# Attention and two expert layers in emulated fp32: another gate function in the first layer, four operand rooms in its second product, later weight sets

## The chip, the cores and the metric

The kernel runs on one core of a Trainium2 chip. A core has TensorE (PE, matmuls into PSUM, the accumulator memory of eight banks), VectorE (DVE), ScalarE (ACT), GpSimd (POOL) and SyncE (SP), which here issues all DMAs, in one queue. The metric is the time of one execution on the device, in microseconds; lower is better.

## The reference

An attention over a compressed memory, then two expert layers, on 8 batches x 576 positions = 4608 tokens of width 512.

```python
# q, k, v: (8, 8, 576, 64); phi: (8, 8, 576, 32); all float32
a = exp(phi - max(phi, axis=2)); a /= sum(a, axis=2) + 1e-9
k_m = einsum('bhsm,bhsd->bhmd', a, k);  v_m = einsum('bhsm,bhsd->bhmd', a, v)
scores = q @ k_m.T / sqrt(64)
attn = softmax(scores, axis=-1);        x = attn @ v_m      # -> (4608, 512)
# layer 1: w_in (512, 2048), w_out (2048, 512), float64
h = x @ w_in;  g = h * sigmoid(1.702 * h);  x = g @ w_out
# layer 2: the same shapes, its own weights
h = x @ w_in;  g = h * sigmoid(h);          out = g @ w_out
```

## The kernel before, in words

Every product is done as three matmuls of a high and a low part (`PASSES`: high x high, high x low, low x high); a tile's high part is a rounded copy made by ACT, its low part the difference, made by DVE or POOL. The weights come as float64 and are converted on the chip: ACT scales both halves (`wconv0`), DVE shifts and sets the sign, POOL adds (`wconv1`). There are four large products, one behind the other.

**First product** (`first1`, 256 steps, 32 a batch). Not attn·v_m and then w_in, but w' = v_m·w_in is made per batch (`wp_mm`, four sets of 512 columns, tiles `slab`) and multiplied with the softmax (`attnT`). A step is six matmuls of 288 columns into one of four PSUM banks, then the gate: ACT takes Tanh of 0.851 h (L326), DVE forms (tanh + 1)·h (L327), which is twice h·sigmoid(1.702 h). Each pair of steps fills one of five `g` buffers, which `g_store` sends to `gs` in DRAM. Between the steps stands the attention of the next batch (`plan_attention`): max over phi, exp of phi (L186), the k/v product (`kv_mm`, 144 matmuls in the trace), transposes of q, the scores, and their softmax with its exp (L270); and the w' sets (`plan_wprime`: matmuls, then `wp_hi` on ACT and `wp_lo` on DVE). Each piece is put in a list under a step number and a place in the step: "e" ahead of the step's matmuls, "p" and "l" behind them, "d" for DMAs. The loop over the steps emits these lists, and the order of each engine's queue is the order of emission. Nothing else decides it.

**Second product** (`first2`, 168 units of 12 matmuls of 384 columns). It is a Strassen-Winograd form: seven products for each of six blocks of 768 tokens, four units (quarters of the inner dimension) a product. A unit's left operand is made from fetched `g` tiles (`r`, `rr`, four quadrants of a block) by `a_prep`: an ACT cast (high part) and a DVE difference (low part, L64) into one of `ROOMS`. Two of the first product's three rooms lie where the attention's buffers were, the third (`op3`) over the first product's `slab` and `g` buffers. `make(0, ROOMS[0], t + 2)` stands ahead of unit t. Results leave through `evac2` (ACT copy times 0.25, DVE sum) to `xs` in DRAM.

**Third product** (`step1`, 48 steps of seven products, L604), gated by one ACT instruction, Silu (L614). **Fourth product** (`prod2`, L666), which is the second's form with other operands, made three units ahead; its fourth quadrant's `r` tiles are fetched ahead of its loop, behind the third product.

The second layer's weights are converted during the second and third product, sent to DRAM (`w2s`), fetched again as sums of blocks (`w_fetch`) and made into seven tiles a set (`w_sums`, `w_high`, `w_low`). Sets (0,0) and (0,1) of the third product are made in the second's last 28 units (`LAST`), (0,2) and (0,3) in the third product. The first layer's `w_out` is loaded and converted in the first product (`w_convert`); its last set goes through `wos` tiles and `wo_move`.

On SP each DMA waits for the DMA eight before it, so the order of issue matters there as it does on the engines.

## Time and profile before

| | |
|---|---|
| time, median of 3 runs | 1513.67 us (1511.62 to 1515.62) |
| profiled execution, its own time | 1512.86 us |
| its span | 1511.1 us |
| PE busy | 1415.0 us, 94% |
| PE weight loads busy | 1334.0 us, 88% |
| DVE busy | 1046.9 us, 69% |
| ACT busy | 788.8 us, 52% |
| POOL busy | 216.1 us, 14% |

The span is the time from the first to the last instruction of the profiled execution; the rest of its own time lies around it. "Busy" is the sum over an engine's instructions. A TensorE that waits inside a stream for its operands, or runs at a lower granted clock, counts as busy in long entries, so 94% isn't 94% of its peak: a stretch has to be compared with the same matmuls in a stretch that waits for nothing. The first product takes the span's first 393.7 us, the second the next 393.8, the third 356, the fourth the rest.

### The profile page before, as it was taken

How to read it: one execution, taken by the hardware profiler on the slowest of the kernel's cores; microseconds unless marked ns; L12 is line 12 of the kernel's file. 1: busy time of each engine (PE TensorE's matmuls, PEld its weight loads, DVE VectorE, ACT ScalarE, POOL GpSimd, SP SyncE). 2: the span in 40 equal slices, each digit the busy share in tenths (PEclk: the TensorE clock that was granted, in tenths of full speed). 3: DMA queues.
4: the chain of work that ended last, by engine and by line, in shares of the span. 5: the costliest groups of instructions: out<-in, count | busy, mean ns of one | idle time of the engine just before them, and what ended most of it. 6: DMA issues, size and time to landing. Idle time of an engine off the chain costs nothing.

```text
span 1511.1 us, 27760 instructions
## 1 busy us (share of the span) xinstructions
PE 1415.0 (94%) x10776; PEld 1334.0 (88%) x10776; DVE 1046.9 (69%) x1513; ACT 788.8 (52%) x1408; POOL 216.1 (14%) x209
## 2 busy tenths in 40 slices
...
GB/s 307 183 189 210 270 246 231 263 174 174 281 35 224 166 158 261 101 223 202 80 99 165 191 194 215 152 212 200 136 210 183 198 43 178 172 50 199 114 107 33
DMA packets 195300, 265.54 MB, mean 176 GB/s; under 512 B 50528, under 2 KB 158048, under 8 KB 195168
## 3 DMA queue, kind: packets, MB, share of 16 engines
...
q8 instruction: 84, 1.38, 0.4%
q14 instruction: 48, 0.39, 0.1%
...
## 4 chain that ended last, share of the span: by engine, by line
PE 69%; DVE 12%; DMA 5%; ACT 5%; issue 4%; POOL 1%; SPq 1%; ACTq 0%; DVEq 0%; POOLq 0%
PE p L666 23%; PE xb L604 13%; PE p L516 12%; PE y L604 10%; PE h L321 8%; DVE op L64 4%; DMA gs<-g 2%; PE aa L240 2%; DVE rr L64 2%; ACT op L499 1%; PE a L196 1%; DMA rr<-gs 1%; DVE o L531 1%; ACT g L326 1%; DVE r L64 1%
## 5 line engine op out<-in xcount | busy, mean ns | idle before, releaser
L516 PE MATMUL p<-op,wq 128*128 128x384 f32 x2016 | 366.1, 341 | 28.0 <-ACT op L499 16.7
L516 PEld LDWEIGHTS p<-op,wq 128*128 128x128 f32 x2016 | 353.6, 190 | 40.2 <-DVE op L64 20.9
L666 PE MATMUL p<-wq,op 128*128 128x256 f32 x3024 | 360.1, 282 | 5.4 <-ACT o L680 3.0
L666 PEld LDWEIGHTS p<-wq,op 128*128 128x128 f32 x3024 | 359.7, 191 | 6.0 <-ACT o L680 3.2
L499 ACT CAST op<-rr 128x768 fp32r<-128x768 f32 x216 | 178.2, 834 | 199.3 <-PE p L666 80.5
L64 DVE TENSOR_TENSOR op<-rr,op 128x768 fp32r<-128x768 f32 x216 | 210.0, 976 | 93.8 <-ACT op L499 92.8
L321 PEld LDWEIGHTS h<-attnT,slab 128*128 128x128 f32 x1536 | 217.0, 195 | 50.5 <-issue 21.9
L321 PE MATMUL h<-attnT,slab 128*128 128x288 f32 x1536 | 248.3, 312 | 14.0 <-DVE g L327 5.2
L604 PE MATMUL xb<-xq,wq 128*128 128x384 f32 x1152 | 216.5, 336 | 0.9 <-DVE e L61 0.5
L604 PEld LDWEIGHTS xb<-xq,wq 128*128 128x128 f32 x1152 | 201.4, 188 | 1.6 <-DVE e L61 0.8
L327 DVE SCALAR_TENSOR_TENSOR g<-g,h 128x288 f32<-128x288 f32 x256 | 110.7, 445 | 98.5 <-ACT g L326 97.9
L604 PE MATMUL y<-xq,wq 128*128 128x384 f32 x864 | 166.6, 337 | 0.7 <-DVE xq L64 0.6
L64 DVE TENSOR_TENSOR op<-r,op 128x768 fp32r<-128x768 f32 x120 | 116.8, 976 | 59.8 <-ACT op L499 59.7
L499 ACT CAST op<-r 128x768 fp32r<-128x768 f32 x120 | 99.7, 834 | 108.9 <-PE p L666 43.9
L604 PEld LDWEIGHTS y<-xq,wq 128*128 128x128 f32 x864 | 151.7, 188 | 1.5 <-DVE xq L64 0.8
L326 ACT ACTIVATE g<-h 128x288 f32<-128x288 f32 x256 | 102.8, 419 | 90.8 <-PE h L321 70.6
L104 POOL TENSOR_TENSOR wst<-wst 128x512 int32<-128x512 int32 x24 | 34.6, 1443 | 496.5 <-DVE wst L102 422.3
L61 DVE TENSOR_TENSOR e<-e,y 128x384 f32<-128x384 f32 x96 | 52.9, 552 | 60.2 <-PE y L604 56.1
L614 ACT ACTIVATE gq<-e 128x384 f32<-128x384 f32 x144 | 75.8, 527 | 15.0 <-DVE e L61 14.8
L61 DVE TENSOR_TENSOR e<-e,xb 128x384 f32<-128x384 f32 x48 | 26.6, 554 | 76.7 <-PE xb L604 70.9
L427 ACT CAST wq<-wst 128x512 fp32r<-128x512 f32 x83 | 51.1, 617 | 35.3 <-DVE wst L64 20.4
L629 ACT COPY e<-xb 128x384 f32<-128x384 f32 x48 | 23.0, 480 | 57.9 <-PE xb L604 57.9
(117 smaller groups left out, 1290.5 us busy)
## 6 DMA issues: line engine op xcount, KB each, us to landing
rr<-gs SPq DMA_DIRECT2D x120, 384.0 KB, 6.5
gs<-g SPq DMA_DIRECT2D x128, 288.0 KB, 4.1
...
```

Source lines behind the costliest of these rows:

```text
L61: eng.tensor_tensor(out=out, in0=a, in1=b, op=ALU.add)
L64: eng.tensor_tensor(out=out, in0=a, in1=b, op=ALU.subtract)
L104: nc.gpsimd.tensor_tensor(out=z, in0=z, in1=low, op=ALU.add)
L321: nc.tensor.matmul(out=h, lhsT=slab[b, f // 4, g][:, wi, f0:f0 + 128], rhs=x[:, g, xi], start=(g == 0 and n == 0), stop=(g == 1 and n == 2))
L326: nc.scalar.activation(out=t, in_=h, func=ACTF.Tanh, scale=0.851)
L327: nc.vector.scalar_tensor_tensor(out=t, in0=t, scalar=1.0, in1=h, op0=ALU.add, op1=ALU.mult)
L427: nc.scalar.copy(out=t[:, :, 0], in_=wst[m, c, k])
L499: nc.scalar.copy(out=t[:, :, 0], in_=s)
L516: nc.tensor.matmul(out=out[:, d, :HB], lhsT=w[:, s, wi, d * 128:(d + 1) * 128], rhs=t[:, s, gi], start=(start and p == 0 and s == 0 and n ...
L604: nc.tensor.matmul(out=out, lhsT=w[:, s, wi, f0:f0 + 128], rhs=x[:, s, xi], start=(start and s == 0 and n == 0), stop=(s == 1 and n == 2), ...
L614: nc.scalar.activation(out=t, in_=h, func=ACTF.Silu, scale=2.0)
L666: nc.tensor.matmul(out=out[:, d], lhsT=t[:, u, gi, d * 128:(d + 1) * 128], rhs=w[:, u, wi], start=(start and d != 1 and p == 0 and u == 0 ...
```

## The change

- The first layer's gate becomes one ACT instruction, Silu(2x), which gives the twofold gate directly. For that the factor 0.851 (`GATE`) is put into `kv_norm`, and taken out again in the softmax's scale and in the second product's evacuation. Silu and exp (with Tanh) lie in different tables of ACT, so each exp is between two table loads. The two exp of the scores of one batch and the two halves of the next batch's phi exp are put at neighbouring steps; a gate between exps that are at most `gap` = 8 steps apart stays Tanh and product (9 of 256). There are 18 table loads for 2 before.
- All step numbers of the first product stand in one table, `PLAN`, with other values; phi's max, difference and exp go in halves, and the start is one list.
- Fetches for the second product: five in the last steps, six and `wo_move` behind them.
- The second product has four operand rooms for three, makes operands three units ahead for two, and has three output tiles for four.
- Weight set (0,1) is made in the third product's first steps, with it (0,2) and (0,3) and what follows are later; the x blocks are fetched 14 products later.
- Ahead of the fourth product, the fourth quadrant is fetched in the third product's last full step, and the third operand made four products later.

```diff
+    GATE = 1.702 / 2
...
-        nc.scalar.activation(out=t, in_=h, func=ACTF.Tanh, scale=0.851)
-        nc.vector.scalar_tensor_tensor(out=t, in0=t, scalar=1.0, in1=h, op0=ALU.add, op1=ALU.mult)
+        if any(lo <= u < hi for lo, hi in exps):
+            nc.scalar.activation(out=t, in_=h, func=ACTF.Tanh)
+            nc.vector.scalar_tensor_tensor(out=t, in0=t, scalar=1.0, in1=h, op0=ALU.add, op1=ALU.mult)
+        else:
+            nc.scalar.activation(out=t, in_=h, func=ACTF.Silu, scale=2.0)
...
-        return pools["mb"].tile([128, 2, HB], F32, tag="o", name="o2", bufs=4)
+        return pools["mb"].tile([128, 2, HB], F32, tag="o", name="o2", bufs=3)
...
-        nc.scalar.activation(out=out, in_=a[:, :, :HB], func=ACTF.Copy, scale=0.25)
+        nc.scalar.activation(out=out, in_=a[:, :, :HB], func=ACTF.Copy, scale=0.25 / GATE)
...
+             3: {'phi': [-29, -28],
+                 'kv': [-35, -32, -29, -26, -23, -21, -14, -14],
+                 'pm': [-25, -25],
+                 'mt': -22,
+                 'mr': -21,
+                 'mb': -21,
+                 'sb': [-19, -18],
+                 'ex': [-17, -16],
+                 'es': -14,
+                 'mm': -4,
...
+                    [[151, 150, 157, 160], [156, 159, 165, 167], 173], [[216, 218, 222, 225], [222, 224, 227, 230], -3]],
+             'w3': [6, 6, 7, 7],
...
+             'rf': [19, 20, 21, 22, 23, 2],
...
+             'w0': [3, 4, 5, 6, 7, 8, 9, 1, 3, 5, 7, 9, 11, 13, 16, 18, 20, 22, 24, 26, 28, 30, 32, 34, 36, 38, 40, 42],
+             'wf': [0, 11, 1, 15],
...
+        if fn in (phi_exp, soft_exp, OPS["ex"], OPS["exp"]):
+            near = [x for x in exps if x[0] - PLAN["gap"] <= slot <= x[1] + PLAN["gap"]]
+            for x in near:
+                exps.remove(x)
+            exps.append((min([slot] + [x[0] for x in near]), max([slot] + [x[1] for x in near])))
...
+        for hf in range(2):
+            y = x["soft"][hf]
+            at(z + y[0], "p", scores, b, hf)
+            at(z + y[1], "e", soft_t, b, hf)
+            at(z + y[2], "e", soft_max, b, hf)
+            at(z + y[3], "e", soft_sub, b, hf, (nc.vector, nc.gpsimd)[x["se"][2 * hf]])
...
+    w1_load(0, 0, 0)
+    w1_load(1, 1, 0)
...
-    for kk in range(4):
-        w1_load(kk, kk, 0)
+    w1_load(2, 2, 0)
+    w1_load(3, 3, 0)
...
-    at(z + 19, "d", swap_pools)
-    for n, (qq, p) in enumerate(((0, 0), (0, 1), (0, 2), (1, 0), (1, 2), (2, 0), (3, 0), (2, 1), (2, 2), (2, 3), (3, 2))):
-        at(z + 19 + n, "d", r_fetch, 0, 0, qq, p)
-    at(z + 29, "d", wo_move)
+    at(z + PLAN["sw"], "d", swap_pools)
+    for n, (qq, p) in enumerate(((0, 0), (0, 1), (1, 0), (0, 2), (1, 2))):
+        at(z + PLAN["rf"][n], "d", r_fetch, 0, 0, qq, p)
...
-    ROOMS = ((("xp", "x1"), ("xp", "x2"), ("mb", "op3")),
+    ROOMS = ((("xp", "x1"), ("xp", "x2"), ("mb", "op3"), ("mb", "op4")),
...
+    AHEAD = 3
...
-    for c, s in enumerate((0, 11)):
-        at(LAST + s, "d", w_fetch, 0, c, "wst")
-        for n in range(7):
-            at(LAST + s + 3 + n, "e", w_sums, 0, c, n, nc.vector)
-            at(LAST + s + 3 + n, "e", w_high, 0, c, n)
-            at(LAST + s + 3 + n, "l", w_low, 0, c, n, nc.vector)
-    at(LAST + 22, "d", w_fetch, 0, 2, "wst")
+    for n in range(7):
+        x = LAST + PLAN["w0"][n]
+        at(x, "e", w_sums, 0, 0, n, nc.vector)
+        at(x, "e", w_high, 0, 0, n)
+        at(x, "l", w_low, 0, 0, n, nc.vector)
+    at(LAST + PLAN["wf"][0], "d", w_fetch, 0, 0, "wst")
+    at(LAST + PLAN["wf"][1], "d", w_fetch, 0, 1, "wst")
...
+    for n, (qq, p) in enumerate(((2, 0), (3, 0), (2, 1), (2, 2), (2, 3), (3, 2))):
+        if n == PLAN["rf"][5]:
+            wo_move()
+        r_fetch(0, 0, qq, p)
...
-        if t + 2 < NS:
-            make(0, ROOMS[0], t + 2)
+        if t == 0:
+            make(0, ROOMS[0], 2)
+        if t + AHEAD < NS:
...
-    spread(0, 2, range(3, 17, 2))
-    at1(2, 4, w_fetch, 0, 3, "wst")
-    spread(0, 3, range(25, 39, 2))
+    for c in (1, 2, 3):
+        spread(0, c, PLAN["w0"][7 * c:7 * c + 7])
+    at1(*divmod(PLAN["wf"][2], 7), w_fetch, 0, 2, "xr")
+    at1(*divmod(PLAN["wf"][3], 7), w_fetch, 0, 3, "wst")
...
-        at1(n + 2, 2, x_fetch, b)
+        at1(n + 4, 2, x_fetch, b)
         for j in range(4):
-            at1(n + 3 + j, 3, x_comb, b, j, nc.vector)
+            at1(n + 5, 1 + 2 * j if j < 3 else 6, x_comb, b, j, nc.vector)
...
+    for p in range(4):
+        at1(NG1 - 1, 2 + p // 2, r_fetch, 1, 0, 3, p)
...
-    at1(NG1, 2, make, 1, ROOMS[1], 2)
+    at1(NG1, 6, make, 1, ROOMS[1], 2)
...
-    for p in range(4):
-        r_fetch(1, 0, 3, p)
```

On ACT, in the first product's fourth batch, stand the exp of that batch's scores (`nat`, out of `soft_exp`) and of the next batch's phi, between gates (`g<-h`), casts of w' (`slab`), of attention (`attnT`) and of `w_out` sets (`wq`). Before, one of the two exps of scores, and phi's, with gates and casts on all sides:

```order
L326 ACTIVATE g<-h 128x288 x2
L288 CAST attnT<-at 128x2x288
L270 ACTIVATE nat<-nat 128x576
L326 ACTIVATE g<-h 128x288
L427 CAST wq<-wst 128x2x256
L326 ACTIVATE g<-h 128x288 x3
L186 ACTIVATE phi<-phi 128x1152
L427 CAST wq<-wst 128x2x256
L326 ACTIVATE g<-h 128x288 x2
L305 CAST slab<-aa 128x512 x2
```

The exps stand alone, four steps apart. In the changed kernel:

```order
L348 ACTIVATE g<-h 128x288
L286 ACT_TABLE_LOAD
L286 ACTIVATE nat<-nat 128x576
L201 ACTIVATE phi<-phi 128x576
L345 ACTIVATE g<-h 128x288
L286 ACTIVATE nat<-nat 128x576
L201 ACTIVATE phi<-phi 128x576
L348 ACT_TABLE_LOAD
L348 ACTIVATE g<-h 128x288
L448 CAST wq<-wst 128x2x256
```

The group of exps stands between two table loads, with one Tanh gate inside it; the casts are elsewhere.

On SP, at the end of the first product, stand the stores of the gates (`gs<-g`), the fetches for the second product (`r`, `rr`) and the move of the last `w_out` set (`wst<-wos`). Before:

```order
L331 DMA gs_5_90<-g 128x576
L474 DMA r<-gs_1_86 128x2x384
L474 DMA r<-gs_2_87 128x2x384
L331 DMA gs_6_91<-g 128x576
L474 DMA r<-gs_3_88 128x2x384
L474 DMA rr<-gs_6_91 128x2x384
L474 DMA rr<-gs_7_92 128x2x384
L397 DMA wst<-wos 128x1024 x2
L331 DMA gs_6_91<-g 128x576
L331 DMA gs_7_92<-g 128x576 x2
L525 DMA xs<-o_5497 128x2x384
```

The last three stores stand behind the fetches and the move. In the changed kernel:

```order
L495 DMA rr<-gs_7_92 128x2x384
L352 DMA gs_5_90<-g 128x576 x2
L352 DMA gs_6_91<-g 128x576 x2
L352 DMA gs_7_92<-g 128x576 x2
L495 DMA r<-gs_0_85 128x2x384
L495 DMA rr<-gs_4_89 128x2x384
L495 DMA rr<-gs_5_90 128x2x384
L418 DMA wst<-wos 128x1024 x2
L495 DMA r<-gs_1_86 128x2x384
L495 DMA r<-gs_2_87 128x2x384
L495 DMA r<-gs_3_88 128x2x384
```

The last stores moved ahead of the move and of six of the fetches.

On SP, between the third and the fourth product, stand the third's gate stores (`gs<-gq`) and the fetches for the fourth. Before:

```order
L616 DMA gs_7_100<-gq 128x384
L474 DMA rr<-gs_0_93 128x2x384
L474 DMA rr<-gs_1_94 128x2x384
L616 DMA gs_3_96<-gq 128x384
L616 DMA gs_7_100<-gq 128x384
L474 DMA rr<-gs_2_95 128x2x384
L474 DMA rr<-gs_3_96 128x2x384
L474 DMA r<-gs_4_97 128x2x384
L474 DMA r<-gs_5_98 128x2x384
L474 DMA r<-gs_6_99 128x2x384
L474 DMA r<-gs_7_100 128x2x384
L675 DMA out_dram<-o_12347 128x3x256
```

The fetches into `r` stand behind all stores. In the changed kernel:

```order
L637 DMA gs_7_100<-gq 128x384
L637 DMA gs_3_96<-gq 128x384
L495 DMA r<-gs_4_97 128x2x384
L495 DMA r<-gs_5_98 128x2x384
L637 DMA gs_3_96<-gq 128x384
L495 DMA r<-gs_6_99 128x2x384
L495 DMA r<-gs_7_100 128x2x384
L495 DMA rr<-gs_2_95 128x2x384
L495 DMA rr<-gs_3_96 128x2x384
L637 DMA gs_7_100<-gq 128x384
L495 DMA rr<-gs_4_97 128x2x384
L495 DMA rr<-gs_5_98 128x2x384
```

The four fetches of gs 4 to 7 into `r` moved from behind the last store to a place ahead of two stores and of the last `rr` fetches.

## Rows read from the trace of the kernel before

**Rows 1.** busy time by stretch (us): engines, clock, DMA share, GB/s
```profile
35.08:103.42 68.34, 53.43 (x479) 40.08 (x479) 48.48 (x83) 35.83 (x79) 27.04 (x26) 0.86 0.65 200
103.42:148.38 44.96, 41.11 (x461) 33.05 (x460) 30.74 (x66) 24.67 (x60) 16.04 (x23) 0.92 0.63 207
148.38:318.74 170.36, 156.98 (x1861) 129.08 (x1860) 126.99 (x272) 107.06 (x256) 93.01 (x95) 1.00 0.76 244
318.74:393.74 75.00, 70.54 (x699) 60.04 (x699) 49.42 (x110) 43.07 (x102) 20.06 (x15) 0.95 0.59 195
393.74:461.62 67.88, 52.34 (x267) 49.96 (x266) 44.25 (x55) 24.92 (x36) 0.00 (x0) 0.87 0.39 135
461.62:704.78 243.16, 238.37 (x1344) 233.30 (x1344) 199.53 (x224) 121.57 (x162) 27.47 (x16) 1.00 0.52 180
704.78:787.59 82.81, 75.18 (x408) 70.34 (x408) 69.95 (x86) 40.72 (x57) 0.00 (x0) 1.00 0.41 133
787.59:1143.59 356.00, 352.00 (x2018) 350.17 (x2017) 196.24 (x300) 223.97 (x450) 21.81 (x16) 1.00 0.55 186
1143.59:1165.27 21.68, 18.69 (x145) 18.48 (x145) 13.36 (x16) 7.07 (x9) 0.00 (x0) 0.92 0.57 204
820.00:840.00 20.00, 20.00 (x117) 20.00 (x116) 14.04 (x22) 13.22 (x29) 1.32 (x1) 1.00 0.52 170
1200.00:1220.00 20.00, 20.00 (x171) 20.00 (x171) 15.86 (x18) 9.53 (x12) 0.00 (x0) 1.00 0.34 120
```

**Rows 2.** timeline of TensorE, first product: start, length, line, count [idle before]
```profile
305.66 2.64 PE L321 MATMUL h<-attnT,slab 128*128 128x288 f32 x18
...
318.74 2.30 PE L196 MATMUL a<-kv,phi 64*32 64x128 f32 x144
...
343.29 6.62 PE L321 MATMUL h<-attnT,slab 128*128 128x288 f32 x48
```

**Rows 3.** groups by line: count, busy us, mean ns, idle before and releaser
```profile
L327 DVE SCALAR_TENSOR_TENSOR g<-g,h 128x288 f32<-128x288 f32 x256 | 110.7, 445 | 98.5 <-ACT g L326 97.9
L326 ACT ACTIVATE g<-h 128x288 f32<-128x288 f32 x256 | 102.8, 419 | 90.8 <-PE h L321 70.6 <-DMA gs<-g 15.3 <-DVE w L101 2.4
...
L270 ACT ACTIVATE nat<-nat 128x576 f32<-128x576 f32 x16 | 11.0, 689 | 2.0 <-POOL nat L266 1.3 <-DVE nat L266 0.8
...
L186 ACT ACTIVATE phi<-phi 128x1152 f32<-128x1152 f32 (+1 forms) x9 | 9.5, 1060 | 12.2 <-DVE phi L182 12.2
```

**Rows 4.** timeline of ACT, start of the third product
```profile
789.48 0.48 ACT L629 COPY e<-xb 128x384 f32<-128x384 f32 x1 [0.17 <-PE xb L604]
789.98 1.28 ACT L614 ACT_TABLE_LOAD   x1
```

**Rows 5.** timeline of TensorE, then of ACT, end of the first product
```profile
358.42 5.03 PE L321 MATMUL h<-attnT,slab 128*128 128x288 f32 x36
...
380.60 1.09 PE L240 MATMUL aa<-w,kvT 64*32 64x512 f32 x16
...
359.92 0.68 ACT L93 ACTIVATE wos<-raw 128x512 f32<-128x512 f32 x1
...
368.81 0.66 ACT L93 ACTIVATE wos<-raw 128x512 f32<-128x512 f32 x1 [4.90 <-DMA raw<-in_moe_w_out_dram]
```

**Rows 6.** timeline of TensorE around w' set 1
```profile
44.91 1.05 PE L240 MATMUL aa<-w,kvT 64*32 64x512 f32 x4 [0.40 <-POOL w L104]
...
58.49 2.77 PE L321 MATMUL h<-attnT,slab 128*128 128x288 f32 x10 [2.17 <-DVE slab L64]
```

**Rows 7.** timelines of TensorE and SP, start of the second product
```profile
409.93 0.69 PE L516 MATMUL p<-op,wq 128*128 128x384 f32 x1 [11.87 <-ACT op L499]
...
400.88 2.13 SPq L331 DMA_DIRECT2D gs<-g  x3
```

**Rows 8.** waits of TensorE: engine and line waited for, us, times, longest
```profile
PE p L516 <- DVE op L64: 11.0, 24, 1.3
```

**Rows 9.** timeline of DVE, start of the fourth product
```profile
1153.73 0.96 DVE L61 TENSOR_TENSOR rr<-rr,r 128x768 f32<-128x768 f32 x1 [4.36 <-DMA r<-gs]
```

More of the change, by code (lines that the diff above doesn't have):

```diff
@@ L304, in wp_hi @@
         t = slab[b, c, g] = moe.tile([128, 2, 512], F32R, tag="slab", name="slab", bufs=4)
-        nc.scalar.copy(out=t[:, 0], in_=st["wp", b, c][g])
+        a = st["wp", b, c][g]
+        nc.scalar.copy(out=t[:, 0], in_=a)
     def wp_lo(b, c, g):
@@ L703, in evac @@
             o_store(b, 1, 0, t)
+    PLAN = {1: {'phi': [0, 2],
+                 'kv': [4, 5, 6, 7, 8, 9, 9, 10],
+                 'pm': [4, 6],
+                 'mt': 9,
+                 'mr': 10,
+                 'mb': 10,
+                 'sb': [12, 12],
+                 'ex': [13, 13],
+                 'es': 14,
+                 'mm': 15,
+                 'norm': 17,
[5 rows of a table added]
+                 'soft': [[21, 22, 22, 22, 24, 26, 27, 28, 29, 29], [24, 25, 26, 26, 27, 28, 29, 30, 32, 32]],
+                 'se': [1, 0, 1, 0]},
+             2: {'phi': [-18, -16],
+                 'kv': [-18, -16, -14, -12, -11, -10, -9, -8],
+                 'pm': [-14, -13],
+                 'mt': -12,
+                 'mr': -10,
+                 'mb': -9,
+                 'sb': [-8, -7],
+                 'ex': [-8, -6],
+                 'es': -4,
+                 'mm': -3,
+                 'norm': -1,
[5 rows of a table added]
+                 'soft': [[5, 6, 7, 9, 15, 17, 18, 20, 21, 24], [11, 12, 13, 14, 16, 18, 20, 25, 26, 26]],
+                 'se': [0, 0, 1, 0]},
+             3: {'phi': [-29, -28],
[8 more added lines that the diff above has]
+                 'mm': -4,
+                 'norm': -2,
[5 rows of a table added]
+                 'soft': [[5, 6, 7, 8, 15, 17, 18, 19, 20, 23], [11, 12, 13, 14, 16, 18, 20, 24, 29, 30]],
[14 rows of a table added]
+                       ('wl', 0, 0), ('wh', 0, 1), ('wl', 0, 1), ('exp', 1), ('sum', 1), ('mul', 1, 0), ('back', 1),
[20 rows of a table added]
+             'gap': 8,
+             'w0': [3, 4, 5, 6, 7, 8, 9, 1, 3, 5, 7, 9, 11, 13, 16, 18, 20, 22, 24, 26, 28, 30, 32, 34, 36, 38, 40, 42],
+             'wf': [0, 11, 1, 15],
+             'w2': [[20, 21, 22, 1], [21, 22, 23, 1], [22, 23, 24, 1], [23, 24, 25, 1]],
+             'sw': 19,
+             'mk': [26, 29],
+             'w26': 15}
@@ L762, in plan_wprime @@
-    def plan_wprime(b, c, s):
-        at(s, "p", wp_mm, b, c)
+            at(z + x["kv"][n], "d", load_kv, b, n)
+        for n in range(2):
+            at(z + x["pm"][n], "e", phi_fold, b, "pm", ALU.max, nc.vector, n)
+            at(z + x["sb"][n], "e", phi_sub, b, slice(2 * n, 2 * n + 2))
+            at(z + x["ex"][n], "e", phi_exp, b, slice(2 * n, 2 * n + 2))
+        at(z + x["mt"], "p", phi_max_t, b)
+        at(z + x["mr"], "e", phi_max_r, b)
+        at(z + x["mb"], "p", phi_max_b, b)
@@ L764, in plan_wprime @@
+    def plan_wprime(b, c):
+        x = PLAN["wp"][min(b, 2) - 1][c]
+        at(32 * b + x[0], "p", wp_mm, b, c)
         for g in range(2):
-            at(s + 1, "e", wp_hi, b, c, g)
-            at(s + 2 + (g if s not in (6, 19) else 0), "e", wp_lo, b, c, g)
+            at(32 * b + x[1 + g], "e", wp_hi, b, c, g)
+            at(32 * b + x[3 + g], "e", wp_lo, b, c, g)
     manual = ExitStack()
@@ L799, in attn_moe_moe @@
     vec, pool = nc.vector, nc.gpsimd
-    def soft(hf, eng, *steps):
-        for n in steps:
-            if n == "sub":
-                soft_sub(0, hf, eng)
-            elif n == "mul":
-                soft_mul(0, hf, eng)
-            else:
-                dict(t=soft_t, max=soft_max, exp=soft_exp, sum=soft_sum, back=soft_back, hi=soft_hi, lo=soft3)[n](0, hf)
-    phi_fold(0, "pm", ALU.max, vec)
-    phi_max_t(0)
-    phi_max_r(0)
-    phi_max_b(0)
-    for n in range(2):
-        phi_sub(0, slice(2 * n, 2 * n + 2))
-        phi_exp(0, slice(2 * n, 2 * n + 2))
```

232 lines of the change are left out of this document (105 added, 127 removed), and 46 rows, old and new, of the table PLAN.

## Prediction

> **What bounds the kernel now.** I read it stage by stage. The windows cut the span at the stage borders [rows 1]: TensorE is busy 91 to 99% in most of them, so the question is which of that is work and which is a stretched stream. For that I looked in TensorE's timeline for stretches without a wait. In [rows 2] nothing is waited for between 305.66 and 343.29: 13 steps before the k/v product at 318.74 (13.08 us) and 19 steps behind it (24.55 us) make 32 steps (78 and 114 matmuls there), one whole batch of the first product with its attention for the next batch, in 37.6 us. The 48 matmuls at 343.29 give the bare step: 6.62 us for 8, 0.82 us. Against that price:
>
> - Steps 0 to 31 (35.08 to 103.42, four w' sets): 68.3 us, where 38.5 would do (a batch and three transposes of q more): 29.8 lost, at a granted clock of 0.86.
> - Steps 32 to 62 (to 148.38): 45.0 against 36.8: 8.2 lost.
> - Four batches (to 318.74): 170.4 against 150.6: 19.8 lost, 5.0 a batch.
> - The last 66 steps (to 393.74): 19 steps in 24.55, then 47 x 0.82 and four w' sets at 1.09 [rows 5]: 67.4, against 75.0: 7.6 lost.
>
> The second product needs 20 / 117 = 0.171 us a matmul (window 820:840 of the third, which is never waited for), 344.6 us for 2016. It takes 393.8, in three pieces: some 265 matmuls to 461.62 take 67.9 for 45.3 (22.6 lost), 1344 take 243.2 for 229.8 (13.4 lost), 408 take 82.8 for 69.8 (13.0 lost). The fourth's first 145 take 21.7 where 20 / 171 = 0.117 us each gives 17.0: 4.7 lost. So some 65 us of waiting lie in the first product and 49 in the second, and this change is about both. DVE is 70% busy in the first product, 82% in the middle of the second and 84% in its last piece, ACT 59% in the first [rows 1].
>
> **Part 1: the gate.** 247 of 256 gates become one Silu (9 stay Tanh and product). 247 x 445 ns = 110 us of DVE go [rows 3], out of 255.6 in the first product's four windows. That alone shortens nothing: DVE wasn't the busiest. What shortens is what stands behind DVE: a step's PSUM bank is free after ACT instead of after ACT and DVE, and the w' low halves, the transposes of the scores and the weight conversions no longer queue among gates. I take the Silu at the Tanh's 419 ns, since no row shows one on 288 columns.
>
> Price: the table. There are 18 table loads for 2, 17 of them in the first product. The trace shows one as 1283 ns, starting 0.02 us behind the copy before it [rows 4]: 17 x 1.283 = 21.8 us, ACT goes from 210.6 to 232 busy us of some 330 (70%). A group in the new order (load, exp 0.69, half of phi's exp 0.53, Tanh 0.42, 0.69, 0.53, load) holds ACT for 5.4 us. TensorE meanwhile has three more banks and the one that the Tanh frees: 4 steps; 5.4 us are 4.6 steps at 37.6 / 32 = 1.18, so about 0.7 us shows, and I take 1.0 for a late start. Eight groups: 8 us. Bounds: 0 (all covered) and 8 x 5.4 = 43 us (nothing covered).
>
> The Trainium skill, "ScalarE: Activation LUTs" (What ACT_TABLE_LOAD costs; Table sets), speaks against this part: it says to batch activations by table set and puts a switch at about 2.66 us, a drain of 1.38 beside the 1.28. The load's 1283 ns agree, the drain is not to be seen ahead of the one load that follows an ACT instruction [rows 4]. By the page the 17 loads would hold ACT another 23 us, and fully uncovered the forecast below would be about 1474.
>
> **Part 2: start and plan.** Two of the first w1 blocks load ahead of k and v. Two blocks of 0.52 MB at 321 GB/s (the four-batch window's 244 GB/s at a share of 0.76) delay the k/v product by 3.3 us; in exchange two conversions are done in ACT's and DVE's waiting time. I take +1.5 us for the first full step; bounds -2 and +4. Later, w' set 1 waited for four conversions: its first matmuls at 44.91, next step at 58.49 [rows 6], 13.6 us for 1.1 of w' and about 1.1 of steps. Now half the set's ACT work is done in the start, and the rest goes out in two bunches ahead of step 4. I take 6.5 of these us, and 5 of the other waits of the first 32 steps, where DVE queues held w' and qT: with the start, -10 net. Bounds: 0 (POOL's adds set the pace as before) and -20.
>
> For the next 31 steps and the four batches I halve what is lost and a bit more (the DVE-bound waits go, the k/v product still waits for the copy ahead of it), 65%, and give back 1.0 per table group: 8.2 becomes 3.9, 5.0 becomes 2.8 a batch: -4 and -9. Bounds: nothing, and all of it (-28 for these five batches).
>
> In the last steps ACT waits for raw w_out: conversion at 359.92, its buffer's next at 368.81, 8.9 us [rows 5], and gates stand behind it. From 363.45 on (358.42 and 36 matmuls) 10 steps take until 380.60. The loads now go out at steps 222 and 225 for 227 and 230: 5 steps and a w' are 5.1 us, so ACT still waits some 3.8, of which three free banks hide 2.5. I take 7.6 to 2.6: -5; bounds 0 and -7.
>
> First product with the start: -28.
>
> **Part 3: second product.** Start: the third operand room lies over the first product's gate buffers, so its cast waits for their last stores. TensorE stands 11.9 us until 409.93; the last three stores go out at 400.88, behind eleven fetches and the move of w_out [rows 7]. Now five fetches (8 transfers, as 16 before) and then all stores go out first. 8 x 0.39 + 7 x 0.295 = 5.2 MB from step 243 on at those 321 GB/s take 16 us, of which 13 steps of 0.82 lie ahead of the end: 6 us after the end, cast 0.83 and low half 0.98 on top, minus two units already made (24 x 0.171 = 4.1): 3.7 us of standing (a delay of the last gates, which wait for older stores, is in it). With some half clock (before: 0.87 over that window) and DVE's adds, 22.6 becomes 9: -13.5. Bounds -5 and -20. Room four waits for the very last store, but has two units more.
>
> Steady part: 13.4 lost over four blocks of 60.8 us, in short waits for the operand's low half from DVE (24 in the whole stage, none over 1.3 us [rows 8]). Operands are now made three units ahead instead of two: 2.06 us more slack. Output tiles go from 4 to 3, but only three are alive at once. I take 13.4 to 4: -9.5; bounds 0 and -13.
>
> Last block: DVE is busy 70.0 of 82.8 us. A whole weight set (11 DVE operations of 0.69, 7 casts) moves to the third product: 7.6 us go, 62.4 are left for 69.8 of TensorE. But x's operands still crowd the last six units. 13.0 to 4.5: -8.5; bounds -3 and -12. In the third product DVE is 55% busy, ACT 63%; the set costs nothing there (2 us if that cover fails). For it the next x block is fetched 14 steps later, six steps (6.2 us) ahead of its first use; were it late, DVE and the sums behind it would stand 1 or 2 us, once or twice.
>
> Second product: -31.5.
>
> **Part 4: fourth product.** DVE waits 4.4 us for r at 1153.73 [rows 9], fetched only behind the third product; an evacuation stands behind that, and TensorE with it. The four fetches now go out in the third product's last full iteration; on SP they pass two others, which land 4 x 0.39 MB or 4.9 us later and are used ten steps on. 4.7 becomes 1: -3.7; and the third operand is made behind the last gates, not ahead of them, one 0.83 us cast: -0.8. Together -4.5; bounds 0 and -6.
>
> **Sum.** The profiled execution took 1512.9 (span 1511.1): 1512.9 - 28 - 31.5 - 4.5 = 1448.9. The median of the three runs is 0.8 above the profiled one: 1449.7, I say 1450.
>
> **Rivals.**
> Tables on the path: the waits on DVE go, but the eight groups are not covered. For it: a load stands in order behind its own step's matmuls and ACT also carries casts of w' and weights; against: ACT is idle 41% and TensorE has four banks. By the page's advice on batching by set it would go this way. 1450 + 43 - 8 = 1485; half of it 1468.
>
> ACT takes DVE's place (the slow side): gates wait for ACT's queue as they did for DVE's, none of the 28 comes, and all groups show: +43 - 31.5 - 4.5 = +7, 1521. It decides where a group shows more than 36 / 8 = 4.5 us with nothing won beside it. For it: of ACT's idle time ahead of gates 70.6 us are waits for TensorE [rows 3], so its room isn't free at any moment one likes; against: in the four batches ACT works 107 of 170 us.
>
> The rooms do little: DVE's rate bounds the second product, its debt passes to the third. Start -8, steady -2, last block -3: 1450 + 18.5 = 1468. For it: DVE is busy 82 to 84%; against: it would have to be near 100%, and the losses are short waits.
>
> Better: nearly all losses of the first product's batches go: 1430.
>
> **Chances.** Forecast (1438 to 1462) 0.58; rooms do little 0.14; tables half or fully on the path 0.14; better 0.07; ACT in DVE's place 0.05; everything cancelled 0.02. 0.3% of 1513.7, 4.5 us, is about what can be told from no change. Faster 0.93, same 0.02, slower 0.05. Range: 1428 to 1480, which leaves out the slow side, half of the table rival's upper half and a little below.
>
> **What would show it.** Right: a batch near 40 us between k/v products; table groups of 5 to 6 us on ACT with TensorE pauses near 1 us; a pause of 3 to 5 us at the start of the second product instead of 12; 58 to 59.5 us per block of 336 matmuls there; no ACT-copy wait at the start of the fourth. Wrong: pauses over 3 us at each table group; blocks still at 60.8; the first product's clock below 0.9 after step 32; a third product longer than 360.

## The result, and the profile after

The changed kernel takes 1473.5 us (median of 4; 1471.1 to 1478.9) for 1512.6 beside it: a ratio of 0.9745, 95% interval 0.9712 to 0.9777. That is faster and inside the range, but 39 us faster and not the 63 of the forecast, and 11 us above the 1438 to 1462 that the forecast gave itself.

First the windows of the changed kernel, each cut at a stage's first matmul: the first product's steps 0 to 31, 32 to 62, 63 to 191 and 192 to 255, then the second product in three pieces (22, 112 and 34 units), then the third. Columns as in [rows 1]. There the k/v product next to a cut stands behind it, here ahead of it, so the pieces of the first product in [rows 1] don't hold the same matmuls as these; the row that stands by itself is steps 63 to 191 of the kernel before, cut as here.

```profile
33.45:102.95 69.50, 53.17 (x629) 39.47 (x630) 45.68 (x79) 43.07 (x87) 29.33 (x32) 0.95 0.70 208
102.95:141.57 38.62, 37.32 (x462) 30.95 (x461) 19.28 (x37) 25.33 (x58) 10.03 (x12) 1.00 0.82 257
141.57:313.99 172.42, 156.16 (x1869) 129.86 (x1868) 90.56 (x162) 119.94 (x269) 84.98 (x86) 0.98 0.74 239
313.99:380.08 66.09, 64.25 (x544) 54.62 (x543) 26.94 (x43) 44.70 (x102) 16.53 (x12) 0.97 0.59 204
380.08:436.36 56.28, 50.60 (x267) 48.86 (x266) 42.80 (x51) 24.14 (x35) 0.00 (x0) 0.94 0.49 171
436.36:675.83 239.47, 236.11 (x1346) 233.28 (x1345) 204.03 (x226) 122.67 (x163) 29.80 (x16) 1.00 0.54 184
675.83:748.18 72.35, 71.49 (x409) 70.91 (x408) 63.07 (x75) 36.37 (x48) 0.00 (x0) 1.00 0.41 131
748.18:1106.16 357.98, 352.15 (x2017) 350.19 (x2016) 192.55 (x309) 227.47 (x455) 25.73 (x16) 1.00 0.56 188
```

```profile
151.13:322.01 170.88, 157.68 (x1872) 130.05 (x1869) 125.07 (x267) 105.45 (x252) 91.70 (x94) 1.00 0.77 248
```

For the comparison between kernels, the first product is cut at the first matmul of steps 32, 63 and 192, by counting its matmuls, six a step, in each run's own profile. Cut so, a k/v product lies in the same stage in every kernel:

| us | to step 0 | steps 0-31 | 32-62 | 63-191 | 192-255 | second | third | fourth |
|---|---|---|---|---|---|---|---|---|
| before | 32.9 | 76.1 | 42.2 | 170.9 | 71.7 | 393.9 | 356.0 | 363.1 |
| after | 33.5 | 69.5 | 38.6 | 172.4 | 66.1 | 368.1 | 358.0 | 361.7 |
| gain | -0.6 | 6.6 | 3.6 | -1.5 | 5.6 | 25.8 | -2.0 | 1.4 |
| e1_tanh | 34.6 | 71.6 | 42.9 | 187.5 | 70.0 | 371.4 | 358.5 | 360.6 |
| e2_no_tables | 33.9 | 62.2 | 37.2 | 170.6 | 64.8 | 371.1 | 357.8 | 361.7 |
| e3_old_silu | 33.3 | 66.6 | 38.5 | 158.2 | 66.9 | 394.9 | 356.0 | 364.1 |
| e4_three_rooms | 34.3 | 66.7 | 38.5 | 169.8 | 66.3 | 380.2 | 358.0 | 361.3 |
| e5_set01 | 34.1 | 67.4 | 38.6 | 172.8 | 64.9 | 375.3 | 358.6 | 360.5 |
| e6_late_r | 34.0 | 69.0 | 38.6 | 174.7 | 64.7 | 367.3 | 357.9 | 365.3 |
| e7_timed | 33.6 | 72.4 | 44.0 | 168.0 | 63.7 | 370.9 | 357.9 | 361.8 |
| e9_old_middle | 33.7 | 67.1 | 45.2 | 189.1 | 65.7 | 371.5 | 357.6 | 362.1 |
| e10_free_first | 34.0 | 68.9 | 38.5 | 170.1 | 62.6 | 368.4 | 357.8 | 360.8 |
| e11_copy_first | 34.5 | 67.4 | 38.6 | 175.7 | 66.1 | 370.2 | 358.4 | 361.0 |
| e12_both | 33.3 | 66.6 | 38.5 | 169.8 | 62.5 | 371.7 | 357.3 | 360.8 |
| e13_free_no_tables | 33.8 | 63.2 | 37.1 | 161.7 | 62.4 | 369.3 | 357.9 | 360.9 |

Kernels with the same code in a stage still differ in it: by 6 us in steps 0 to 31 (66.6 to 72.4 in the nine with the new step table, its gate and its table loads) and in steps 63 to 191 (169.8 to 175.7 in after, e4, e5, e6 and e11), by 4 in the second product (367.3 to 371.5 where nothing in it was altered), by 1 or 2 elsewhere. A smaller stage difference from one profile each says little.

The surprise stands in one column: the four middle batches, from which 9 us were expected, gave none. DVE got its relief there (90.6 busy us in 172.4, for 125.1 in 170.9), and nothing came of it. The gate's lines, which answer to [rows 3]:

```profile
L348 ACT ACTIVATE g<-h 128x288 f32<-128x288 f32 x247 | 98.2, 420 | 77.2 <-PE h L339 59.4 <-issue 6.4 <-DMA gs<-g 3.6
...
L348 ACT ACT_TABLE_LOAD x9 | 11.5, 1283 | 2.1 <-DMA gs<-g 2.0
...
L286 ACT ACT_TABLE_LOAD x7 | 9.0, 1283 | 0.1
...
L346 DVE SCALAR_TENSOR_TENSOR g<-g,h 128x288 f32<-128x288 f32 x9 | 4.1, 451 | 17.1 <-ACT g L345 17.1
```

247 Silu at 420 ns, as taken; 16 of the first product's 17 loads stand in these rows at 1283 ns.

### The profile page after: what moved, and what is told of

Its sections match the earlier page's. It is cut to its first block, busy times and chain, and to the rows that moved or that the text cites. A ratio compares the mean times of both kernels' runs of the same rounds, so it can differ in the third digit from the quotient of the medians.

```text
span 1472.3 us, 27420 instructions
## 1 busy us (share of the span) xinstructions
PE 1396.1 (95%) x10776; PEld 1326.8 (90%) x10776; DVE 963.1 (65%) x1299; ACT 812.2 (55%) x1429; POOL 207.0 (14%) x193
## 3 DMA queue, kind: packets, MB, share of 16 engines
q8 instruction: 84, 1.38, 0.4%
## 4 chain that ended last, share of the span: by engine, by line
PE 78%; DMA 7%; DVE 5%; ACT 3%; issue 1%; SPq 1%; POOL 0%; ACTq 0%; DVEq 0%
PE p L687 23%; PE p L537 17%; PE xb L625 13%; PE h L339 11%; PE y L625 10%; PE aa L256 2%; DMA xs<-o 1%; DMA rr<-gs 1%; DVE op L65 1%; PE a L211 1%; DMA q<-in_q_dram 1%; SPq L495 1%; DMA gs<-g 1%; PE a L244 1%; DVE r L62 1%
## 5 line engine op out<-in xcount | busy, mean ns | idle before, releaser
L537 PE MATMUL p<-op,wq 128*128 128x384 f32 x2016 | 358.4, 339 | 9.9 <-DVE op L65 4.5
L339 PE MATMUL h<-attnT,slab 128*128 128x288 f32 x1536 | 239.2, 307 | 18.3 <-ACT g L348 14.0
L65 DVE TENSOR_TENSOR op<-rr,op 128x768 fp32r<-128x768 f32 x216 | 209.0, 974 | 66.2 <-ACT op L520 65.5
L339 PEld LDWEIGHTS h<-attnT,slab 128*128 128x128 f32 x1536 | 212.9, 193 | 41.6 <-ACT g L348 20.5
L65 DVE TENSOR_TENSOR op<-r,op 128x768 fp32r<-128x768 f32 x120 | 123.2, 1031 | 73.8 <-ACT op L520 73.7
L348 ACT ACTIVATE g<-h 128x288 f32<-128x288 f32 x247 | 98.2, 420 | 77.2 <-PE h L339 59.4
L111 POOL TENSOR_TENSOR wst<-wst 128x512 int32<-128x512 int32 x24 | 40.9, 1704 | 488.4 <-DVE wst L105 279.5
L65 DVE TENSOR_TENSOR slab<-aa,slab 128x512 fp32r<-128x512 f32 x62 | 39.8, 680 | 45.1 <-ACT slab L322 42.8
L65 DVE TENSOR_TENSOR wq<-wst,wq 128x512 fp32r<-128x512 f32 x63 | 43.0, 687 | 13.4 <-ACT wq L448 13.3
```

The source lines that it names most:

```text
L65: eng.tensor_tensor(out=out, in0=a, in1=b, op=ALU.subtract)
L111: nc.gpsimd.tensor_tensor(out=z, in0=z, in1=parts(t, dst)[0], op=ALU.add)
L339: nc.tensor.matmul(out=h, lhsT=slab[b, f // 4, g][:, wi, f0:f0 + 128], rhs=x[:, g, xi], start=(g == 0 and n == 0), stop=(g == 1 and n == 2))
L348: nc.scalar.activation(out=t, in_=h, func=ACTF.Silu, scale=2.0)
L537: nc.tensor.matmul(out=out[:, d, :HB], lhsT=w[:, s, wi, d * 128:(d + 1) * 128], rhs=t[:, s, gi], start=(start and p == 0 and s == 0 and n ...
```

## The experiments

**The gate alone, both ways.** The new step table with the old gate, and the old step table with the new one.

```diff
 e1_tanh (from after)
-        if any(lo <= u < hi for lo, hi in exps):
+        if True:
 e2_no_tables (from after): Silu in place of every exp, so one table
-        if any(lo <= u < hi for lo, hi in exps):
+        if False:
-        nc.scalar.activation(out=t, in_=t, func=ACTF.Exp)
+        nc.scalar.activation(out=t, in_=t, func=ACTF.Silu)
 e3_old_silu (from before): the gate one Silu, the exps as in e2
```

e1_tanh: 

> All 256 gates of the first product are Tanh and product again, everything else as in the changed kernel; its exps then stand in the gate's table, so ACT loads 2 tables instead of 18, and DVE gets 247 products of 0.445 us back (110 us). Theory A (Silu won in the four middle batches what was forecast, and the table groups took it again): the two cancel, 1473 within 4, with DVE waits in place of the table pauses. Theory B (DVE did not hold these batches; they wait for late transfers, and for ACT at the groups): the tables' pauses of 1.1 to 1.3 us in eight groups go and nothing comes back, 1463 to 1466. Theory C (the new step table only works with a light DVE): 1485 or more, steps in the middle batches held by the gate's product.

Measured: 1504.5 us, ratio 0.9948 (0.9928 to 0.9967). Theory C: 31 us slower than after, 15 of it in the middle batches. There TensorE's waits (engine and line waited for: us, times, longest) are DVE's:

```profile
PE h L339 <- DVE g L346: 12.3, 12, 4.1
PE aa L256 <- DVE slab L65: 7.4, 9, 1.7
PE aa L256 <- DVE nat L274: 3.0, 1, 3.0
```

So the Silu, with all its table loads, is worth 31 us in this step table.

e2_no_tables: 

> All gates are Silu and every exp of the attention is computed with the Silu function instead (the exp is left out, so that ACT has one table): the price of the tables by themselves, with the 9 remaining products of DVE. Theory A: 1473 less the forecast's 13 us or more, 1450 to 1460. Theory B: less eight pauses of about 1.2 us, 1462 to 1466. If the tables were hidden altogether: 1473 within 3.

Measured: 1464.8, ratio 0.9699 (0.9669 to 0.9728): 8.6 us for the tables, theory B's size. The two intervals of the ratio make this good to some 6 us. The middle batches still took 170.6 us.

e3_old_silu: 

> The kernel before with nothing changed but the gate: one Silu instead of Tanh and product, and the exps computed with the Silu function too (exp left out, the gate's factor not folded), so no tables: what 256 products less on DVE are worth in the old order. Theory A (DVE's queue held the first product): 25 us or more below 1512, at 1488 or less, of it 5 a batch. Theory B (DVE was not what held it): at most 6 us, 1506 to 1512.

Measured: 1485.0, ratio 0.9822 (0.9797 to 0.9846): 27 us faster than before, theory A's size, though with 3 us a batch for its 5. The second product starts at 363.5 for 393.7 us. Here the middle batches took 158.2 us, 12 less than in e2_no_tables, though both have Silu and no tables:

```profile
138.43:296.64 158.21, 153.84 (x1872) 129.12 (x1869) 78.18 (x137) 106.12 (x252) 91.57 (x93) 1.00 0.82 267
```

```profile
133.38:303.95 170.57, 156.80 (x1869) 130.08 (x1868) 90.65 (x158) 109.83 (x261) 84.94 (x86) 0.97 0.76 243
```

The first row is the old step table, the second the new one: DVE is busy 78 and 91 us; in the new one TensorE stands 9.4 us more and is 3.0 us longer busy with the same matmuls. DVE did hold the middle batches; the new step table then loses there what the Silu wins. (The expectations of e9 and e13 take 160.5 and 170.5 for these two: the cut behind the 160.5 lies one k/v product earlier, so that it holds five of them and the 170.5 four. The difference is 12 us and not 10.)

**What the new table loses.** In the changed kernel's trace the conversions of `w_out` come too early after their loads. First ACT around step 64, then TensorE, then two windows behind the pause:

```profile
148.78 0.66 ACT L94 ACTIVATE wst<-raw 128x512 f32<-128x512 f32 x1 [2.98 <-DMA raw<-in_moe_w_out_dram]
...
149.91 1.29 ACT L348 ACTIVATE g<-h 128x288 f32<-128x288 f32 x4
```

```profile
150.35 1.09 PE L339 MATMUL h<-attnT,slab 128*128 128x288 f32 x6 [2.47 <-ACT g L348]
...
153.12 1.81 PE L339 MATMUL h<-attnT,slab 128*128 128x288 f32 x6
...
155.05 1.03 PE L339 MATMUL h<-attnT,slab 128*128 128x288 f32 x6
```

```profile
150.30:151.40 1.10, 1.05 (x6) 0.84 (x6) 1.10 (x3) 0.90 (x3) 0.64 (x1) 1.00 0.90 361
151.90:154.90 3.00, 2.92 (x24) 2.02 (x25) 1.58 (x4) 0.00 (x0) 0.15 (x1) 0.50 1.05 394
```

ACT waits 3.0 us for a `raw` tile, four gates stand behind it, TensorE pauses 2.5 us, and from 151.9 us on the granted clock is 0.50 for 3 us: six matmuls take 1.81 us where 1.03 is usual. A second place, at a table group (SP, ACT, TensorE):

```profile
198.67 0.70 SPq L150 DMA_DIRECT2D kv<-in_v_dram  x1
207.94 0.33 SPq L77 DMA_DIRECT2D raw<-in_moe_w_out_dram  x1
```

```profile
208.04 0.39 ACT L348 ACTIVATE g<-h 128x288 f32<-128x288 f32 x1
208.46 1.28 ACT L286 ACT_TABLE_LOAD   x1
209.75 0.69 ACT L286 ACTIVATE nat<-nat 128x576 f32<-128x576 f32 x1
...
214.46 1.28 ACT L348 ACT_TABLE_LOAD   x1 [2.00 <-DMA gs<-g]
215.75 0.71 ACT L348 ACTIVATE g<-h 128x288 f32<-128x288 f32 x2
```

```profile
216.21 4.97 PE L339 MATMUL h<-attnT,slab 128*128 128x288 f32 x24 [3.31 <-ACT g L348]
```

SP issues nothing from 199.4 to 207.9 with a `raw` load at its head, whose buffer comes free when POOL ends the first conversion of the set (206.59 and 1.31 us); the stores behind it are late, so a gate's `g` buffer is late, the table load that stands ahead of that gate waits 2.0 us, and the group's pause is 3.3 us instead of the 1.1 to 1.3 of the other groups. SP stood at that load before as well (5.4 us, until 212.85); but there each third load had nine steps until its own conversion. Now the first set has three, and in the second set the conversion that frees the buffer stands at step 108 instead of 106.

```diff
 e7_timed (from after)
-  [[53, 56, 62, 64], [62, 64, 65, 72], 73]
+  [[53, 55, 60, 63], [57, 59, 66, 69], 73]
   ... conversions 156 -> 157; 227, 230 -> 229, 233; last q a step earlier
 e10_free_first (from after)
+  [[53, 56, 64, 66], [62, 64, 70, 73], 75]
+  [[100, 101, 110, 112], [106, 108, 116, 119], 123]
+  [[150, 151, 160, 162], [156, 158, 166, 169], 175]
+  [[216, 218, 224, 226], [222, 224, 230, 233], -3]   ... last q as in e7
 e13_free_no_tables: e10_free_first and e2_no_tables together
```

e7_timed: 

> The changed kernel with a few numbers of the step table altered, where its trace shows transfers arriving late: the w_out tiles loaded and converted at steps 53, 55, 60, 63 and 57, 59, 66, 69 (the third had three steps between load and conversion), the last ones converted at 229 and 233, and the last q tile of a batch loaded a step earlier. Theory B2 (the middle batches lose in the new table by late transfers, each pause followed by a stretch at the lower clock): steps 32 to 63 and the four batches together some 6 to 8 us shorter, last steps 3, in all 1463 to 1467. Rival (the late transfers are hidden behind something else, such as the order of the attention's steps): 1471 to 1475.

Measured: 1475.0, ratio 0.9742 (0.9713 to 0.9772): no gain. The last steps gained 2.4, the batches 4.4 (less than their scatter), and steps 32 to 62 lost 5.4: now a conversion waits in front of the k/v product. ACT, then TensorE there:

```profile
142.41 0.66 ACT L94 ACTIVATE wst<-raw 128x512 f32<-128x512 f32 x1 [2.01 <-DMA raw<-in_moe_w_out_dram]
...
144.27 3.86 PE L211 MATMUL a<-kv,phi 64*32 64x128 f32 x142 [3.38 <-ACT qT L248]
```

e9_old_middle: 

> The changed kernel with the step numbers of before for the batches from the fourth on, for w' from the third batch on and for the first three w_out sets; only the exps stand grouped (steps 20 and 21 of a batch), and the Silu gate, the start, the first batches and all later stages stay as changed. In the old order with Silu and without tables the four middle batches took 160.5 us, in the new one without tables 170.5. Theory (the new step table itself costs these 10 us): four batches at 160 to 164, the whole at 1461 to 1466. Rival (the old order only did well because it had no table groups in it): 169 to 172, the whole at 1471 to 1476.

```diff
 e9_old_middle (from after): PLAN[3], 'wp' from batch 2, 'wo' of sets 0 to 2
+  'soft': [[6, 7, 8, 9, 20, 22, 22, 24, 25, 26], [14, 15, 16, 17, 21, 23, 24, 27, 28, 29]]
   ... other numbers as in before, phi's exp at -12, -11
```

Measured: 1494.1, ratio 0.9876 (0.9850 to 0.9903), batches at 189.1: worse than either. It answers nothing on the old order, since grouping the exps at steps 20 and 21 made a chain of its own: ACT, DVE and POOL at one such place:

```profile
187.14 0.67 ACT L304 CAST attnT<-at 128x576 fp32r<-128x576 f32 x1 [4.82 <-DVE at L300]
...
186.32 0.78 DVE L300 STREAM_TRANSPOSE at<-nat 128x576 f32<-128x576 f32 x1 [8.19 <-POOL attnT L65]
...
180.01 3.69 POOL L175 TENSOR_TENSOR es<-es,phi 128x128 f32<-128x128 f32 x7
...
184.90 1.40 POOL L65 TENSOR_TENSOR attnT<-at,attnT 128x576 fp32r<-128x576 f32 x1
```

The exps' tail was too late: POOL's sum over phi (3.7 us) stands ahead of the low part, whose end frees `at` for DVE's transpose, and ACT's cast and all gates behind it wait 4.8 us.

e10_free_first: 

> The changed kernel with the w_out steps of the first product rewritten so that a raw buffer is free when the load into it comes up: in each set the third and fourth load stand two or more steps behind the conversion that frees their buffer, and six steps ahead of their own (loads 53, 56, 64, 66 and conversions 62, 64, 70, 73, and so on for the four sets); the last q tile a step earlier. In the changed kernel's trace SP issued nothing from 198.7 to 207.9 us, with a raw load at the head of its queue and stores and q loads behind it. Theory B2 (this standing on SP is the 10 us that the new table costs in the middle batches): steps 63 to 96 and 96 to 128 about 5 us shorter each, the four batches at 161 to 165, the last steps at 64, the whole at 1459 to 1464. Rival (the late transfers were hidden, or the pauses go elsewhere, as when the first conversions were put earlier): 1470 to 1475.

Measured: 1467.3, ratio 0.9690 (0.9663 to 0.9716): 6 us better, between the theory and the rival, with 3.5 of it in the last steps; the batches at 170.1 miss their 161 to 165. The edit does what it was made for: SP no longer stands at a `raw` load in the batches (8.6 us at the place above). That brought the batches little until both edits were put together.

e13_free_no_tables: 

> The w_out steps of the previous study (buffers free ahead of their loads) together with Silu in place of every exp (exp left out, one table). It tells what is left of the 10 us by which the new step table, without tables of ACT, was slower in the four middle batches (170.5) than the old one (160.5). Theory (late transfers and table groups hide one another: with either there the same pauses come, without both they go): four batches at 160 to 164, the whole at 1450 to 1455. Rival (the order of the attention's and w' steps itself costs the rest): four batches at 166 to 170, the whole at 1457 to 1461.

Measured: 1452.5, ratio 0.9596 (0.9572 to 0.9620). The batches, with e10 first and e13 second:

```profile
141.39:311.47 170.08, 156.22 (x1869) 130.46 (x1868) 91.20 (x162) 120.38 (x269) 84.10 (x86) 0.98 0.75 243
```

```profile
134.16:295.81 161.65, 154.41 (x1869) 129.73 (x1868) 89.67 (x158) 109.62 (x261) 84.16 (x86) 0.98 0.79 256
```

| steps 63-191, us | with tables | without |
|---|---|---|
| w_out as changed | 172.4 | 170.6 |
| buffers free first | 170.1 | 161.7 |

Each cause taken away alone gives about 2 us, which one profile can't tell from nothing; both together 10.7, which it can. In whole times: 8.6 and 6.2 alone, 21.0 together. Late transfers and table groups hide one another. One place shows it: without the tables but with the old loads (e2_no_tables), ACT gets to the late `raw` tile of step 64 sooner and waits 4.7 us for it instead of 3.0, and TensorE pauses 4.1 us instead of 2.5:

```profile
142.26 0.66 ACT L94 ACTIVATE wst<-raw 128x512 f32<-128x512 f32 x1 [4.68 <-DMA raw<-in_moe_w_out_dram]
```

```profile
143.84 1.81 PE L339 MATMUL h<-attnT,slab 128*128 128x288 f32 x6 [4.14 <-ACT g L348]
```

With both gone the new order comes in the batches within 3.5 us of the old one (158.2), which is less than the scatter.

**The second product.**

```diff
 e4_three_rooms (from after)
-    ROOMS = ((("xp", "x1"), ("xp", "x2"), ("mb", "op3"), ("mb", "op4")),
+    ROOMS = ((("xp", "x1"), ("xp", "x2"), ("mb", "op3")),
-    AHEAD = 3
+    AHEAD = 2                       ... 3 again for the fourth product
 e5_set01 (from after): w0's steps of set (0,1) at LAST + 14 to LAST + 20
```

e4_three_rooms: 

> The changed kernel with three operand rooms and operands two units ahead in the second product; stores first, three output tiles and the late weight set stay. If the fourth room and the third unit ahead are what shortened the steady blocks (60.8 to 59.4 us each) and part of the last block: 1473 + 5 for the blocks + 3 at the start + 3 at the end, about 1484. Rival (the order of fetches and the moved set did it, DVE's rate sets the blocks): 1473 within 3.

Measured: 1484.0, ratio 0.9813 (0.9790 to 0.9835), as the theory had it. The second product is 12.1 us longer; the 112 units from unit 28 on take 243.1 us, as before (243.2), for 239.5 in the changed kernel, and the last 28 take 64.9 for 59.8. The first 22 take 57.9, for 56.3 in the changed kernel and 66.2 before, so most of the start's gain doesn't come from the rooms. TensorE's waits in the whole stage, changed kernel first (it answers to [rows 8]):

```profile
PE p L537 <- DVE op L65: 4.5, 9, 0.6
```

```profile
PE p L537 <- DVE op L65: 10.2, 20, 1.3
PE p L537 <- ACT op L520: 5.3, 6, 1.7
```

The fourth room and the third unit ahead, which this edit takes back together, halve both count and length of the waits for the low half.

e5_set01: 

> The changed kernel with weight set (0,1) made in the second product's last 28 units again, at the steps of before. Theory (the set's 11 operations of 0.69 us on DVE were what the last units waited for): the last block goes from 61 to about 69 us and the time to 1478 to 1481, less what the third product's start gives back (1 to 2 us). Rival (operands three units ahead cover DVE there, so the move was free): 1473 within 3.

Measured: 1482.9 with a wide spread (1475.1 to 1489.8), ratio 0.9808 (0.9760 to 0.9856). By the traces the last 28 units take 66.0 us for 59.8: the set costs 6 there, as the theory had it, and the third product gives nothing back (358.6).

e11_copy_first: 

> The changed kernel with the copy out of the first product's bank emitted ahead of the operand three units on, once in the second product and once in the fourth (first block, unit 6). The trace shows TensorE waiting 2.8 and 1.7 us for this copy, which stands on ACT behind a cast that waits for DVE's sums. If the queue on ACT is what costs: 4.5 us less, 1468 to 1470. Rival (DVE's sums set these units, TensorE waits for the operand instead): 1473 within 2.

```diff
 e11_copy_first (from after; the same in the fourth product)
-        if t + AHEAD < NS:
+        if t + AHEAD < NS and (b, i, p) != (0, 1, 3):
             make(0, ROOMS[0], t + AHEAD)
...
             evac2(b, i, bank)
+            if (b, i) == (0, 1):
+                make(0, ROOMS[0], t + AHEAD)
```

In the changed kernel, TensorE and ACT at the start of the second product:

```profile
385.63 0.44 PE L537 MATMUL p<-op,wq 128*128 128x384 f32 x1 [1.22 <-ACT op L520]
...
403.80 8.12 PE L537 MATMUL p<-op,wq 128*128 128x384 f32 x36 [2.81 <-ACT o L549]
```

```profile
382.61 0.71 ACT L348 ACTIVATE g<-h 128x288 f32<-128x288 f32 x2 [3.21 <-DMA gs<-g]
...
398.41 0.83 ACT L520 CAST op<-r 128x768 fp32r<-128x768 f32 x1 [3.58 <-DVE r L65]
402.21 0.83 ACT L520 CAST op<-r 128x768 fp32r<-128x768 f32 x1 [2.96 <-DVE r L65]
402.94 0.80 ACT L549 ACTIVATE o<-p 128x768 f32<-128x768 f32 x1
```

The copy at 402.94 stands behind two casts that wait for DVE's sums, and TensorE waits 2.8 us for it. Measured: 1474.2, ratio 0.9741 (0.9716 to 0.9765): the rival. Unit 8 started 2.9 us earlier (20.8 us behind unit 0 for 23.7), and by unit 28 it was gone (68.8 for 68.8); in the fourth product the 1.7 us wait for the copy went too, and the stage takes 361.0 for 361.7. In the second, TensorE, without the copy's wait, waits for the operands:

```profile
406.31 2.18 PE L537 MATMUL p<-op,wq 128*128 128x384 f32 x11 [0.55 <-DVE op L65]
409.09 0.44 PE L537 MATMUL p<-op,wq 128*128 128x384 f32 x1 [0.60 <-ACT op L520]
```

e12_both: 

> Both of these edits together: the sum of what they bring, 1455 to 1460 if both theories hold, 1466 to 1472 if one of them does, 1473 if none does.

Measured: 1466.8, ratio 0.9696 (0.9672 to 0.9720): e10_free_first's gain alone, as follows from the above. These two are the best that compute the whole reference.

**The fourth product.**

```diff
 e6_late_r (from after)
-        at1(NG1 - 1, 2 + p // 2, r_fetch, 1, 0, 3, p)
+    for p in range(4):            # behind the third product
+        r_fetch(1, 0, 3, p)
```

e6_late_r: 

> The changed kernel with the fourth quadrant of the fourth product fetched behind the third product again. The forecast took 3.7 us for this; the trace of the changed kernel shows the start only 1.4 us shorter, with DVE waiting 1.7 us for an rr tile in place of the r tile and the same evacuation late. Theory (the wait went from one fetch to the next in the queue): at most 2 us slower, 1473 to 1476. Rival (the early fetch is worth its 3.7 us and something else was lost): 1477 or more.

Measured: 1478.7, ratio 0.9773 (0.9758 to 0.9787): 5 us slower than after, the fourth product 365.3 for 361.7. The rival: the early fetch is worth 3.6 us there. DVE and TensorE of the changed kernel (it answers to [rows 9]), then of this one:

```profile
1115.07 0.96 DVE L62 TENSOR_TENSOR rr<-rr,r 128x768 f32<-128x768 f32 x1 [1.67 <-DMA rr<-gs]
```

```profile
1126.61 3.58 PE L687 MATMUL p<-wq,op 128*128 128x256 f32 x29 [1.72 <-ACT o L701]
```

```profile
1117.15 0.96 DVE L62 TENSOR_TENSOR rr<-rr,r 128x768 f32<-128x768 f32 x1 [4.85 <-DMA r<-gs]
```

```profile
1128.69 1.61 PE L687 MATMUL p<-wq,op 128*128 128x256 f32 x9 [2.46 <-ACT o L701]
```

DVE's wait is 1.7 us for an `rr` tile instead of 4.9 for an `r` tile, and TensorE's 1.7 instead of 2.5. Without the early fetch the fourth product would have been 2.2 us slower than before, so another edit lost about that. Whether it was the later third operand or the later weight set was not tried, and stays open.

## Why the prediction came out as it did

- **The step that failed: the gain of the first product, -28, measured -13.7** (its end moved from 393.7 to 380.1). In it, "For the next 31 steps and the four batches I halve what is lost and a bit more" stands for -4 and -9, and measured -3.6 and +1.5: it is the batches that failed. The reason given, that DVE-bound waits go, was right: in the old step table the Silu alone took 30.2 us off the first product, 12.7 of them in the batches (e3). What it left out is the w_out loads of the middle, which the prediction followed in the last steps only. Three sets had moved nearer to their conversions or behind a later one, and those pauses, with the lower clock behind them, together with the table groups filled what the Silu had opened. e13 shows the forecast's mechanism with both out of the way: the first product ends at 358.2, 35.5 us earlier, where the forecast without its 8 us for the tables has 36.
- **The price of the tables: 8, measured 8.6** (e2), or 14.8 where the transfers are in time (1467.3 to 1452.5, of it 5.7 in the first 32 steps and 8.4 in the batches). The agreement of 8 and 8.6 is in part luck, since the price doesn't lie where the sum had it. A pause of "1.0 for a late start" a group was right for three of the four groups in the batches (1.1, 1.1, 1.3), and so were the load's 1283 ns; but steps 0 to 31, with two of the eight groups, take 62.2 and 63.2 us without tables and 66.6 or more with them, and the clock behind a pause was not in the sum. The Trainium skill's "ScalarE: Activation LUTs" (What ACT_TABLE_LOAD costs) gives about 2.66 us for a switch, 1.38 of it a drain; the load at 208.46 starts 0.03 us behind the gate ahead of it, so that drain is not seen here. That the 1474 which the prediction works out by this page of the Trainium skill is also the measured time is chance.
- **Start and first 32 steps: -10, measured -6.0** (0.6 later, then 6.6 shorter). The Silu alone takes 9.5 off these 32 steps (e3), the new plan without tables 4.4 more (e2), and the tables take 7.3 back.
- **Last steps: -5, measured -5.6**; e10's later conversions add 3.5: ACT still waited 2.9 and 2.2 us for raw tiles, against the 3.8 that were worked out. (There are 65 steps behind the last k/v product and not 66, so 8.4 us were lost there and not 7.6.)
- **Second product: -31.5, measured -25.8.** Cut at units 22 and 134 in both kernels ([rows 1] cut a few matmuls later), start -13.5, measured -9.9, with the stores ahead of the fetches as in the row below, which answers to [rows 7] (SP: start, length, count); TensorE's standing at the third unit went from 11.9 to 1.2 us, and 2.8 us for the copy came behind it. Steady part -9.5, measured -4.9, a block taking 59.9 us where 58 to 59.5 had been named: waits for the low half fell as they should, yet TensorE's 1344 matmuls keep 9.7 us over the third product's price per matmul. PE stands only 3.4 of them; what stretches the rest stays open. Last block -8.5, measured -11.0: about 6 are the moved set's (e5) and 5 the rooms' (e4), for which the prediction had nothing there.

```profile
375.24 8.42 SPq L352 DMA_DIRECT2D gs<-g  x6
```

- **Third and fourth product: 0 and -4.5, measured +2.0 and -1.4.** The early fetch did its 3.6; TensorE's waits in the third product grew from 4.0 to 6.0 us in all, short ones for ACT's copies at its start and end. e5 puts set (0,1) back and keeps these 2 us, so it isn't that set.

Of the rivals none held whole, though the measured time lies where two of them, tables half on the path and rooms that do little, had theirs. The tables cost 8.6 us and not the 25 or 43 of that rival, and "The rooms do little" fell with e4. DVE's place was not taken by ACT's work (e1 and e3 speak against it) but, in the middle batches, by ACT's standing in line. Not tried is the old order of the attention's steps with the Silu and its table groups: e9 was meant for it, and made a wait of its own.
